# Bucket attention, experts and MLP on one core: the order of transposes and products of P in the attention

## The chip, the cores and the metric

The kernel runs on one core of a Trainium2 chip. The metric is the device time of one execution in microseconds (us). Two kernels are told apart by the ratio of their times over several runs.

## The reference

Three layers follow each other. What the change touches is the first one, an attention with a mask by hash buckets:

```
q, k, v: (2, 8, 768, 64) float32;  proj: (64, 6)
q_bucket, k_bucket = sum over 6 bits of 2**i * ((q or k) @ proj > 0)
scores = q @ k.T / 8, and -1e9 where the buckets of a query and a key differ
attn   = exp(scores - rowmax);  attn /= sum(attn) + 1e-9
x      = attn @ v, heads side by side: (1536, 512)
```

Then a layer of eight experts: a token goes to the expert with the largest router logit (x @ w_gate + a bias by modality), and its output is gate * relu(x @ w1[e]) @ w2[e]. Then an MLP: softplus(x @ w_in) @ w_out with 2048 inner columns. All results are float32, and the kernel computes products in two float32r parts (a high part H and the rest L), so that they are close to float32.

## The kernel before, in words

**Groups and pieces.** The attention works through 48 groups. A group is 256 queries of one head: two tiles of 128. For each tile, TensorE makes scores (pieces S0 and S1, four products each, a tile of two PSUM banks), VectorE takes the row maximum (M0, M1), GpSimd makes scale and bias of the exponent from it, and ScalarE makes the exponentials P with their sums (X0, X1).

P has its queries on the partitions, and the product with v needs its keys there. So TensorE transposes P, 128 x 128 at a time, into PSUM tiles `ps_t` of which there are two. A *bank* is one such tile: two tiles of keys for two tiles of queries, four transposes; a group has three banks (T0, T1, T2). ScalarE casts a bank to P's high part PH (H0, H1, H2), and VectorE subtracts it to get the low part PL (L0, L1, L2). Both read the `ps_t` tile, so it is free for another bank when its L is done.

The product with v (V0, V1, V2, by bank) has v as the stationary operand and PH or PL as the moving one, 256 columns (the two tiles of queries). v is held as 128 columns a head: 64 of its high part and 64 of its low part. PH meets all 128 (a *full* product), PL the 64 of the high part alone (a *narrow* product). For each of the two tiles of keys of a bank the order is full, narrow; the group's last tile of keys has them the other way round. All accumulate in one PSUM tile `ps_o`. ScalarE copies it to SBUF (O), TensorE adds its two halves and gives the router's logits with products of 72 columns (F, four records, into columns that the tile of S1's scores leaves free), and VectorE scales the result by the sums (r).

**Iterations.** Pieces of different groups are interleaved. In iteration `it` the scores are those of group `it`, the transposes those of group `it - 2`, the products with v those of group `it - 3` and F, O and r those of group `it - 4`. Up to iteration 40 there is also R, a piece of the next head pair's preparation (transposes of q or k, or products for the bucket bits), with its readers A on ScalarE and D on VectorE. Each engine has an order of its own, written out by hand:

```
ORDER = ("S0 T0 V0 T1 S1 F V1 T2 R V2", "O X1 H0 H1 X0 H2 A", "M0 L0 M1 L1 r L2 D")
```

These are the orders of TensorE, ScalarE and VectorE. `FIRST` has such lines for iterations 0 to 5, and `DRAIN` for the last four groups and the first work of the experts behind them. `run` and the loop over `DRAIN` issue a piece when those that it needs have been issued (`after`, `needs`); they wait for nothing at run time beyond semaphores for data and buffers. From iteration 28 on some pieces of the routing run in between on VectorE, TensorE and GpSimd.

After the attention come the routing, the experts' slots with their weights split into two parts by ScalarE and VectorE, and the MLP. Lines to follow: `scores` L242, `rowmax` L254, `expo` L265, `tpose_pe` L274 (transposes, L283), `tpose_hi` L286 (L288), `tpose_lo` L290 (L293), `pv` L296 (products, L307), `fin1` L310 (L313), `fin_pe` L323 (L329), `fin_dve` L331 (L338, L344), `prep_pe` L154 (L175).

Of the kernel before, what the change touches and what calls it, by code (L numbers as in the profile page):

```python
# [15 lines left out]
PSUM = bass.MemoryType.PSUM  # L16
P = 128
BIG = 4096.0
RND = 1.5 * 2.0 ** 23  # added and subtracted, it rounds a float32 to the nearest integer
OFF = (P - 1) / 2  # L20


class Attention:
    """Bucket-masked attention, a pair of heads at a time.

    q and k are transposed and split into float32r parts H + L. One K=128 product of [qH; qH] with
    [kH; kL] and one of [qL; bits] with [kH; bits] give the scores: the bit rows add exactly 0 for
    equal buckets and at most -1 (of scores scaled by 2**-32) for others. A row without a match
    has its exponent scaled by 0.
    """  # L30
# [19 lines left out]
    def open(self, ctx, c_p):  # L50
        """ctx: for the whole of the attention; c_p: a pool for constants"""
        self.c_p = c_p
        # what the last pair needs until its operands are made lies on top, and goes first
# [9 lines left out]
        # and so goes what the pair before it takes  # L63
# [37 lines left out]
    # products of zeros: the tensor engine's clock is up when the first operands come  # L101
# [17 lines left out]
    def consts_c(self):  # L119
        nc, c_p, D = self.nc, self.c_p, self.D  # L120
        # sums the two parts of the output, and gives its share of the router logits
        self.wgx = c_p.tile([P, self.H, D + self.E], F32, name="wgx")
        for i in range(2):
            sl = slice(D * i, D * i + D)
            nc.vector.tensor_copy(self.wgx[sl, :, :D], self.ident[sl, sl].unsqueeze(1).to_broadcast([D, self.H, D]))
            nc.scalar.dma_start(out=self.wgx[sl, :, D:], in_=self.wg.rearrange("(h d) e -> d h e", d=D))
# [27 lines left out]
    def prep_pe(self, m, i, ps_of=None):  # L154
        nc, S, HS = self.nc, self.S, self.HS
        if i == 0:
            own = ("qH", "qL", "kH", "kL", "bt")
            self.prep[m] = {}
            if m == 0:
                # in the place of tiles that come later, so that the next pair's need not wait  # L160
# [57 lines left out]
    def head0(self, i):  # L218
        """the first head's operands by the engines, which have nothing else to do yet"""
# [54 lines left out]
    def tpose_pe(self, g, bk):  # L274
        e = self.st[g]
# [4 lines left out]
        for kk in range(2):  # L280
            for t in range(2):
                kt = 2 * bk + kk
                self.nc.tensor.transpose(ps[:, kk, t], e["P"][t][:, kt * P:(kt + 1) * P], self.ident)  # L283
        e["T", bk] = ps.rearrange("p k t n -> p (k t n)")

# [10 lines left out]
    def pv(self, g, bk):  # L296
        m, j, u = self.gm(g)
        e = self.st[g]
        if bk == 0:
            e["O"] = self.ps_m.tile([P, 512], F32, tag="o", name="ps_o")  # L300
        O, vh, NT = e["O"], self.vhl[m], self.NT
        for kt in (2 * bk, 2 * bk + 1):
            ops = [(P, "PH"), (self.D, "PL")]
            if kt == NT - 1:
                ops.reverse()
            for n, nm in ops:
                self.nc.tensor.matmul(O[:n, :2 * P], vh[:, j, kt, :n], e[nm][:, kt], start=(kt == 0 and n == P),  # L307
                                      stop=(kt == NT - 1 and n == P))
# [8 lines left out]
    def spare(self, s):  # L317
        """the columns that a tile of scores leaves free in its two banks, [P, 2, P]"""
# [35 lines left out]
    def run(self, aside, aside_ps, end):  # L354
        """the groups, up to iteration end"""
# [17 lines left out]
        for t in range(4):  # L373
            self.split_v(0, t)
        after = {"M0": ["S0"], "M1": ["S1"], "X0": ["M0"], "H0": ["T0"], "H1": ["T1"], "H2": ["T2"], "L0": ["H0"],
                 "L1": ["H1"], "L2": ["H2"], "F": ["O", "S1"], "R": ["M1"], "r": ["F"], "A": ["R"], "D": ["A"], "S1": ["S0"], "T0": [], "T1": ["T0"],
# [5 lines left out]
        for it in range(end):  # L382
# [7 lines left out]
            # the second pair's operands are made with the first group, while nothing else can be done  # L390
# [6 lines left out]
            def do(k):  # L397
# [9 lines left out]
                elif a == "T" and ok(T_):  # L407
                    self.tpose_pe(T_, n)
                elif a == "H" and ok(T_):
# [20 lines left out]
                # the second pair's operands  # L430
# [31 lines left out]
    # per iteration: the order of the pieces on PE, ACT and DVE  # L462
    LAG = (2, 3, 4)
    ORDER = ("S0 T0 V0 T1 S1 F V1 T2 R V2", "O X1 H0 H1 X0 H2 A", "M0 L0 M1 L1 r L2 D")
    # the first iterations, p, a and d being the second pair's pieces on PE, ACT and DVE
# [11 lines left out]
class Moe:  # L477
    def __init__(self, tc, ctx, ident, mid, wg, mb, w1, w2, win, wout, x_dram, x2_dram, out):
# [10 lines left out]
        # slots: as many as the experts' tokens can take, and the first NA of them, that are always computed  # L489
        self.NS = self.TT + self.E - 1  # L490
        self.NA = self.NS - 2
        # and the first two once more
# [11 lines left out]
    def consts(self, e_p):  # L504
        """a generator; e_p: a pool for what is used up here"""
# [29 lines left out]
        # row of x2 of each slot row, if the slots were full  # L535
# [3 lines left out]
        # id of token b * 768 + p * 6 + t as 64 * (high + 32) + low  # L539
# [19 lines left out]
        # tri[k, m] = 1 where k < m  # L559
# [40 lines left out]
    def bias(self, m):  # L600
        """logits start as the bias of the token's modality: the share of modality m"""
# [29 lines left out]
    # A token takes the slot row slotbase[expert] * 128 + rank, the rank counting its expert's tokens before it.  # L631
    # The generators yield where an engine may do other things in between.
    def route_a(self, b):
        """the expert of each token of batch b, one-hot, and the exponentials that its gate takes"""
# [34 lines left out]
    def ranks(self, R, t0, t1):  # L669
        """adds the ranks that the tokens of columns t0 to t1 bring; R: [P, t, E] of PSUM"""  # L670
# [6 lines left out]
    def place(self, src, t0, t1):  # L677
        """slot (relative where src has no slot bases) and row of the tokens of columns t0 to t1, the row as (row - OFF) / 128"""
# [17 lines left out]
    def gate3(self, eng, t0, t1):  # L696
        """gates as three bfloat16 parts"""
# [11 lines left out]
    # The first slot holds the first tokens of the expert that most tokens of batch 0 go to, and the second one more of them:  # L709
    # where batch 0 has more than 128 of them, as is all but sure, its product can run before batch 1 is done.  # L710
    # Elsewhere it and the second slot write nothing, and come again after the other slots.
    def first_a(self, ps):
        """ranks modulo 128 of batch 0, and its most frequent expert; ps: [P, 2, P] of PSUM"""
# [26 lines left out]
    def first_b(self):  # L740
        """what its tokens bring to the table of the first slot"""
# [24 lines left out]
    def first_c(self):  # L766
        """the order of the experts with that one in front"""
        E, tp, G = self.E, self.tp, self.nc.gpsimd
        # nothing is written by the first two slots
# [11 lines left out]
        # tri[k, m] = 1 where k comes before m  # L781
# [20 lines left out]
    def first_d(self, ps):  # L802
        """token and gate of the first slot's rows; ps: [P, 2, P] of PSUM"""
# [31 lines left out]
    def route_n(self, i):  # L835
        """the slots that come before each expert, into the ranks"""
# [13 lines left out]
        if i == 3:  # L850
            # for the tables that are not needed at once
# [9 lines left out]
    def open_route(self):  # L861
        """the pools on the right that the experts take"""
# [747 lines left out]
```

## Time and profile before

| | |
|---|---|
| median of 3 runs | 784.7 us (782.81 to 785.21) |
| span of the profiled execution | 782.7 us |
| TensorE: products busy / weight loads busy | 757.3 us (97%) / 646.5 us (83%) |
| VectorE, ScalarE, GpSimd busy | 588.3 us (75%), 521.0 us (67%), 282.0 us (36%) |
| attention, about | 5 to 260 us |

The profile was taken from one execution; its own device time is not listed beside the span, and the median of the runs lies 2.0 us above that span. PE is TensorE's row of products and transposes, PEld its row of weight loads, DVE is VectorE, ACT ScalarE and POOL GpSimd. TensorE's instructions overlap: a record opens before the one ahead of it has ended, so the time that one costs is the distance between starts and not the length of a record. Where equal instructions follow each other they stand merged in the timeline, with their first start, the time from that start to the last end, and their count.

### The profile page before, as it was taken

Reading aid. Unit: us, or ns where it says so; the run is one execution under the profiler, and the core shown is the slowest. Engines: PE = TensorE matmul, PEld = TensorE weight load, DVE = VectorE, ACT = ScalarE, POOL = GpSimd, SP = SyncE. Lnnn points to the kernel's source line nnn. Section 1 sums busy time; section 2 is a strip of 40 time slices with the busy share of each in tenths; the row PEclk is TensorE's granted clock in tenths of the full one; section 3 lists DMA queues with packets and bytes.
Section 4 is the critical chain, followed back from the end, with each engine's and each line's share of the span. In section 5 each row is a group of like instructions: output and inputs, shape, how many; then the busy total and the mean of one; then the engine's idle time right before and its main releaser. Section 6 shows DMA issues by size and latency. Waiting matters only on the chain. (4 is left out here: it accounts for less than half of the span.)

```text
span 782.7 us, 13113 instructions
## 1 busy us (share of the span) xinstructions
PE 757.3 (97%) x4225; PEld 646.5 (83%) x4225; DVE 588.3 (75%) x842; ACT 521.0 (67%) x869; POOL 282.0 (36%) x627
## 2 busy tenths in 40 slices
PE   7899999999999999999999999999989999999996
PEld 5799999999999767878878888766668888888874
DVE  6798888898988868999999998899973333433250
ACT  5787787887879568898898898555553333342340
POOL 4455544446565564234432133544441100020001
PEclk9999999999999989999999999999999999999999
DMA  8855647526660013679963642244430100010001
GB/s 195 186 129 121 162 94 165 149 63 170 181 198 22 21 41 130 216 245 340 370 241 110 209 156 68 88 161 165 162 107 24 40 1 1 27 54 1 0 1 54
DMA packets 72602, 95.28 MB, mean 122 GB/s; under 512 B 31843, under 2 KB 48227, under 8 KB 72529
## 3 DMA queue, kind: packets, MB, share of 16 engines
q1 hardware_dynamic: 67152, 83.85, 36.2%
q0 software_dynamic: 3744, 9.45, 3.4%
q10 hardware_dynamic: 1632, 1.08, 0.6%
q8 instruction: 35, 0.57, 0.3%
q14 instruction: 39, 0.31, 0.1%
HBM read 105.18 MB, written 10.76 MB: 148 GB/s over the span
## 5 line engine op out<-in xcount | busy, mean ns | idle before, releaser
L997 DVE TENSOR_TENSOR wL<-wr,wH 128x1024 fp32r<-128x1024 f32 (+1 forms) x134 | 160.9, 1232 | 13.2 <-ACT wH L992 12.9
L992 ACT CAST wH<-wr 128x1024 fp32r<-128x1024 f32 (+1 forms) x144 | 141.4, 1005 | 7.4 <-PE ps_p L1113 2.8
L1304 DVE SCALAR_TENSOR_TENSOR gg<-ps_f,ga 128x512 f32<-128x512 f32 x48 | 33.0, 689 | 108.0 <-ACT ga L1300 108.0
L260 DVE TENSOR_REDUCE mx<-s 128x1 f32<-128x768 f32 x96 | 91.6, 954 | 21.8 <-PE s L329 19.3
L271 ACT ACTIVATE p<-s,nb,sc 128x768 f32<-128x768 f32 x96 | 96.0, 1000 | 15.7 <-POOL nb L262 12.8
L293 DVE TENSOR_TENSOR PL<-ps_t,PH 128x512 fp32r<-128x512 f32 x144 | 98.3, 683 | 7.0 <-ACT PH L288 6.7
L1298 ACT ACTIVATE ga<-ps_f 128x512 f32<-128x512 f32 x48 | 28.7, 598 | 107.1 <-PE ps_f L1296 107.1
L288 ACT CAST PH<-ps_t 128x512 fp32r<-128x512 f32 x144 | 83.9, 589 | 16.6 <-PE ps_t L283 14.1
L250 PE MATMUL s<-K,Q 76*128 76x384 f32 (+1 forms) x384 | 88.2, 350 | 2.4 <-ACT p L271 0.9
L307 PE MATMUL ps_o<-PH,vhl 128*128 128x256 f32 x288 | 86.7, 316 | 0.6 <-ACT Os L313 0.6
L283 PE MATMUL ps_t<-ident,p 128*128 128x128 f32 x576 | 86.4, 272 | 0.6 <-DVE PL L293 0.6
L1296 PE MATMUL ps_f<-x2H,mwL 128*128 128x512 f32 x192 | 77.1, 402 | 3.2 <-POOL mwL L1285 3.2
L1296 PE MATMUL ps_f<-x2H,mwH 128*128 128x512 f32 x192 | 77.1, 401 | 0.1
L1331 PE MATMUL ps_o<-mwH,gL 128*128 128x512 f32 x192 | 76.9, 401 | 0.0
L1296 PE MATMUL ps_f<-x2L,mwH 128*128 128x512 f32 x192 | 76.1, 396 | 0.0
L1331 PE MATMUL ps_o<-mwH,gH 128*128 128x512 f32 x192 | 75.8, 395 | 0.0
L1331 PE MATMUL ps_o<-mwL,gH 128*128 128x512 f32 x192 | 75.8, 395 | 0.0
L283 PEld LDWEIGHTS ps_t<-ident,p 128*128 128x128 f32 x576 | 69.4, 140 | 2.7 <-PE s L250 0.9
L1285 POOL TENSOR_TENSOR mwL<-w,mwH 128x1024 fp32r<-128x1024 f32 x16 | 47.6, 2978 | 62.4 <-ACT mwH L1284 62.4
L307 PE MATMUL ps_o<-PL,vhl 128*64 128x256 f32 x288 | 68.3, 280 | 0.0
L250 PEld LDWEIGHTS s<-K,Q 76*128 76x128 f32 (+1 forms) x384 | 62.9, 189 | 4.0 <-ACT p L271 1.7
L1125 POOL DMA_INDIRECT x_dram<-y,cpi x17 | 23.8, 1397 | 102.1 <-ACT y L1120 70.9
(292 smaller groups left out, 1663.2 us busy)
## 6 DMA issues: line engine op xcount, KB each, us to landing
wr<-in_moe_w_dram SPq DMA_DIRECT2D x136, 512.0 KB
wraw<-in_moe_w_in_dram SPq DMA_DIRECT2D x16, 512.0 KB
wraw<-in_moe_w_out_dram SPq DMA_DIRECT2D x16, 512.0 KB
Q<-qH SPq DMA_DIRECT2D x28, 192.0 KB
K<-kH SPq DMA_DIRECT2D x28, 192.0 KB
rawv<-in_v_dram SPq DMA_DIRECT2D x8, 384.0 KB
x_dram<-x SPq DMA_DIRECT2D x8, 384.0 KB
rawq<-in_q_dram SPq DMA_DIRECT2D x14, 192.0 KB
```

The costliest lines, as they stand in the source:

```text
L250: self.nc.tensor.matmul(s[:, h, :HS], d[l, j][:kk, ts], d[r, j][:kk, h * HS:(h + 1) * HS], start=(a == 0), stop=(a == 1))
L260: nc.vector.tensor_reduce(mx, s[:, :, :self.HS], axis=AX.XY, op=ALU.max)
L271: self.nc.scalar.activation(e["P"][ti].rearrange("p (h c) -> p h c", h=2), s[:, :, :self.HS], AF.Exp, scale=sc, bias=nb, accum_out=e["sum" ...
L283: self.nc.tensor.transpose(ps[:, kk, t], e["P"][t][:, kt * P:(kt + 1) * P], self.ident)
L288: self.nc.scalar.copy(e["PH"][:, 2 * bk:2 * bk + 2].rearrange("p k n -> p (k n)"), e["T", bk])
L293: self.nc.vector.tensor_tensor(e["PL"][:, sl].rearrange("p k n -> p (k n)"), e["T", bk], e["PH"][:, sl].rearrange("p k n -> p (k n)").bitc ...
L307: self.nc.tensor.matmul(O[:n, :2 * P], vh[:, j, kt, :n], e[nm][:, kt], start=(kt == 0 and n == P), stop=(kt == NT - 1 and n == P))
L992: self.nc.scalar.copy(self.wt[s, c][0][:, sl], self.raw[c][:, sl])
L997: eng.tensor_tensor(L[:, sl], self.raw[c][:, sl], H[:, sl].bitcast(F32), op=ALU.subtract)
L1285: nc.gpsimd.tensor_tensor(L, w, H.bitcast(F32), op=ALU.subtract)
L1296: nc.tensor.matmul(ps, w[:, 0, sl], x[:, k], start=(k == 0 and n == 0), stop=(k == self.KD - 1 and n == 2))
L1331: nc.tensor.matmul(self.ops[i], a[:, sl], w[:, 1], start=(f == 0 and n == 0), stop=(f == NF - 1 and n == 2))
```

## The change

Transposes and products of a bank are issued in another order. A new piece W stands for T and V of the same number in one: two transposes, then the bank's four products in their order, each narrow one with a transpose straight ahead of it. So where the order was T T T T full narrow full narrow, it is T T full T narrow full T narrow (in a group's last bank T T full T narrow T narrow full). The transposes are those of group `it - 2`, the products those of group `it - 3`, as before. TensorE's order by iteration has W0, W1 and W2 in place of T and V; with that V1 stands ahead of S1 and F, and R behind the last bank. In `DRAIN` a T that a V follows is issued so too, where that V can be issued, and some V's are moved up behind a T. Comments are dropped.

```diff
     def tpose_pe(self, g, bk):
+        for f in self.tposes(g, bk):
+            f()
+
+    def tposes(self, g, bk):
...
+        def one(kk, t):
+            kt = 2 * bk + kk
+            self.nc.tensor.transpose(ps[:, kk, t], e["P"][t][:, kt * P:(kt + 1) * P], self.ident)
+        return [lambda kk=kk, t=t: one(kk, t) for kk in range(2) for t in range(2)]
+
+    def tpose_pv(self, gt, gv, bk, bv=None):
+
+        ts = self.tposes(gt, bk)
+        ts.pop(0)()
+        ts.pop(0)()
+        for narrow, f in self.pvs(gv, bk if bv is None else bv):
+            if narrow:
+                ts.pop(0)()
+            f()
...
     def pv(self, g, bk):
+        for _, f in self.pvs(g, bk):
+            f()
+
+    def pvs(self, g, bk):
...
+        def one(kt, n, nm):
+            self.nc.tensor.matmul(O[:n, :2 * P], vh[:, j, kt, :n], e[nm][:, kt], start=(kt == 0 and n == P),
+                                  stop=(kt == NT - 1 and n == P))
+        made = []
         for kt in (2 * bk, 2 * bk + 1):
             ops = [(P, "PH"), (self.D, "PL")]
             if kt == NT - 1:
                 ops.reverse()
...
+            made += [(n < P, lambda kt=kt, n=n, nm=nm: one(kt, n, nm)) for n, nm in ops]
+        return made
...
+                elif a == "W":
+                    self.tpose_pv(T_, V_, n)
...
-    ORDER = ("S0 T0 V0 T1 S1 F V1 T2 R V2", "O X1 H0 H1 X0 H2 A", "M0 L0 M1 L1 r L2 D")
+    ORDER = ("S0 W0 W1 S1 F W2 R", "O X1 H0 H1 X0 H2 A", "M0 L0 M1 L1 r L2 D")
...
-        3: ("S0 T0 V0 T1 S1 V1 T2 V2", "X1 H0 H1 X0 H2", "M0 L0 L1 M1 L2"),
-        4: ("T0 S0 V0 T1 S1 F V1 V2 T2", "O X1 H0 H1 X0 H2", "M0 L0 M1 L1 r L2"),
-        5: ("S0 T0 V0 T1 S1 F V1 T2 R V2", "O X1 H0 H1 X0 H2 A", "M0 L0 M1 L1 r L2 D"),
+        3: ("S0 W0 W1 S1 W2", "X1 H0 H1 X0 H2", "M0 L0 L1 M1 L2"),
+        4: ("W0 S0 W1 S1 F W2", "O X1 H0 H1 X0 H2", "M0 L0 M1 L1 r L2"),
+        5: ("S0 W0 W1 S1 F W2 R", "O X1 H0 H1 X0 H2 A", "M0 L0 M1 L1 r L2 D"),
...
-    "S04 T02 V01 T12 S14 F0 V11 T22 V21 S05 T03 V02 T13 S15 F1 V12 T23 V22 S06 T04 V03 V13 T14 S16 F2 T24 x0 V23 S07 T05 V04"
-    " T15 S17 F3 V14 T25 V24 g00 T06 V05 T16 F4 V15 V25 T26 T07 g01 V06 T17 V16 T27 V26 F5 g10 V07 F6 V17 V27 g11 F7 E g20 g21"
+
+    "S04 T02 V01 T12 V11 S14 F0 T22 V21 S05 T03 V02 T13 V12 S15 F1 T23 V22 S06 T04 V03 T14 V13 S16 F2 T24 x0 V23 S07 T05 V04"
+    " T15 V14 S17 F3 T25 V24 g00 T06 V05 T16 V15 F4 V25 T26 T07 g01 V06 T17 V16 T27 V26 F5 g10 V07 F6 V17 V27 g11 F7 E g20 g21"
...
+                if k[0][0] == "T" and len(k) > 1 and k[1][0] == "V" and all(y in done for y in needs(k[1])):
+                    (bt, gt), (bv, gv) = ([int(x) for x in y[1:]] for y in k[:2])
+                    att.tpose_pv(NG - 2 * TAIL + gt, NG - 2 * TAIL + gv, bt, bv)
+                    done.add(k.pop(0))
+                else:
+                    do(k[0])
```

## Rows read from the trace of the kernel before

**Rows 1.** Busy time by engine in a stretch: stretch, its length, then each engine.

```profile
200.00:250.00 50.00, 50.00 (x396) 49.45 (x395) 43.74 (x80) 43.20 (x89) 29.17 (x105) 1.00 0.50 137
```

**Rows 2.** TensorE's waits, 30 to 255 us: total us, times, longest.

```profile
PE ps_o L307 <- ACT Os L313: 0.6, 1, 0.6
```

**Rows 3.** Timeline of TensorE, iteration 44, without R: start us, us, what.

```profile
235.59 0.87 PE L250 MATMUL s<-K,Q 128*128 128x384 f32 x4
236.29 0.60 PE L283 MATMUL ps_t<-ident,p 128*128 128x128 f32 x4
236.65 0.36 PE L307 MATMUL ps_o<-PH,vhl 128*128 128x256 f32 x1
...
237.08 0.28 PE L307 MATMUL ps_o<-PL,vhl 128*64 128x256 f32 x1
237.20 0.60 PE L283 MATMUL ps_t<-ident,p 128*128 128x128 f32 x4
...
238.37 0.56 PE L329 MATMUL s<-wgx,Os 128*128 128x72 f32 x4
...
239.28 0.60 PE L283 MATMUL ps_t<-ident,p 128*128 128x128 f32 x4
...
240.19 0.86 PE L250 MATMUL s<-K,Q 128*128 128x384 f32 x4
```

**Rows 4.** Groups by line and shape, 150 to 330 us: busy us, mean ns.

```profile
L283 PE MATMUL ps_t<-ident,p 128*128 128x128 f32 x268 | 40.1, 272 | 0.0
...
L329 PE MATMUL s_spare<-wgx,Os 128*128 128x72 f32 x16 | 2.4, 274 | 0.0
...
L283 PEld LDWEIGHTS ps_t<-ident,p 128*128 128x128 f32 x268 | 32.2, 141 | 0.8
L307 PEld LDWEIGHTS ps_o<-PH,vhl 128*128 128x128 f32 x142 | 26.8, 189 | 0.3 <-ACT Os L313 0.2
L307 PEld LDWEIGHTS ps_o<-PL,vhl 128*64 128x64 f32 x142 | 18.9, 136 | 0.0
```

**Rows 5.** Timeline of all engines, iteration 37, with a short R.

```profile
200.47 0.88 PE L250 MATMUL s<-K,Q 128*128 128x384 f32 x4
...
200.81 0.68 DVE L293 TENSOR_TENSOR PL<-ps_t,PH 128x512 fp32r<-128x512 f32 x1
...
202.10 0.60 PE L283 MATMUL ps_t<-ident,p 128*128 128x128 f32 x4
...
205.39 0.34 PE L250 MATMUL s<-K,Q 128*128 128x384 f32 x1
```

**Rows 6.** Timeline of two narrow windows, transposes after an idle stretch.

```profile
22.43 0.14 PEld L283 LDWEIGHTS ps_t<-ident,p 128*128 128x128 f32 x1 [0.88 <-PE s L250]
...
22.46 0.41 PE L283 MATMUL ps_t<-ident,p 128*128 128x128 f32 x2 [0.58 <-DVE PL L293]
22.49 0.25 PEld L283 LDWEIGHTS ps_t<-ident,p 128*128 128x128 f32 x2
```

**Rows 7.** Timeline of a narrow window, scores after an idle stretch.

```profile
19.74 0.30 PEld L250 LDWEIGHTS s<-K,Q 128*128 128x128 f32 x2 [0.41 <-ACT p L271]
```

**Rows 8.** Timeline of TensorE, narrow window, F straight behind a transpose.

```profile
256.43 0.38 PE L283 MATMUL ps_t<-ident,p 128*128 128x128 f32 x2
256.65 0.34 PE L329 MATMUL s_spare<-wgx,Os 128*128 128x72 f32 x2
```

**Rows 9.** Timeline of VectorE, iteration 44, without R.

```profile
236.26 0.68 DVE L293 TENSOR_TENSOR PL<-ps_t,PH 128x512 fp32r<-128x512 f32 x1
...
238.97 0.96 DVE L260 TENSOR_REDUCE mx<-s 128x1 f32<-128x768 f32 x1 [0.25 <-PE s L329]
...
240.86 0.68 DVE L293 TENSOR_TENSOR PL<-ps_t,PH 128x512 fp32r<-128x512 f32 x1
```

**Rows 10.** Timeline of all engines, iteration 32, with routing work.

```profile
175.26 0.68 DVE L293 TENSOR_TENSOR PL<-ps_t,PH 128x512 fp32r<-128x512 f32 x1
...
176.03 0.29 PE L283 MATMUL ps_t<-ident,p 128*128 128x128 f32 x1
```

More of the change, by code (lines that the diff above doesn't have):

```diff
@@ L279, in tpose_pe @@
         ps = self.ps_t.tile([P, 2, 2, P], F32, tag="t", name="ps_t")
[L280 to L283, printed above, removed]
         e["T", bk] = ps.rearrange("p k t n -> p (k t n)")
+        def one(kk, t):
[10 more added lines that the diff above has]
+            f()
     def tpose_hi(self, g, bk):
@@ L305, in pv @@
                 ops.reverse()
-            for n, nm in ops:
-                self.nc.tensor.matmul(O[:n, :2 * P], vh[:, j, kt, :n], e[nm][:, kt], start=(kt == 0 and n == P),
-                                      stop=(kt == NT - 1 and n == P))
+            made += [(n < P, lambda kt=kt, n=n, nm=nm: one(kt, n, nm)) for n, nm in ops]
+        return made
     def fin1(self, g):
@@ L374, in run @@
             self.split_v(0, t)
-        after = {"M0": ["S0"], "M1": ["S1"], "X0": ["M0"], "H0": ["T0"], "H1": ["T1"], "H2": ["T2"], "L0": ["H0"],
-                 "L1": ["H1"], "L2": ["H2"], "F": ["O", "S1"], "R": ["M1"], "r": ["F"], "A": ["R"], "D": ["A"], "S1": ["S0"], "T0": [], "T1": ["T0"],
+        after = {"M0": ["S0"], "M1": ["S1"], "X0": ["M0"], "H0": ["T0", "W0"], "H1": ["T1", "W1"], "H2": ["T2", "W2"], "L0": ["H0"],
+                 "L1": ["H1"], "L2": ["H2"], "W1": ["W0"], "W2": ["W1"], "F": ["O", "S1"], "R": ["M1"], "r": ["F"], "A": ["R"], "D": ["A"], "S1": ["S0"], "T0": [], "T1": ["T0"],
                  "T2": ["T1"], "V1": ["V0"], "V2": ["V1"], "X1": [], "X0": ["M0", "X1"], "M1": ["S1", "M0"], "V0": [], "p4": ["d0", "d1"]}
@@ L1569 @@
                 k = next(x for x in todo if x and all(y in done for y in needs(x[0])))
-                do(k[0])
+                if k[0][0] == "T" and len(k) > 1 and k[1][0] == "V" and all(y in done for y in needs(k[1])):
[4 more added lines that the diff above has]
+                    do(k[0])
                 done.add(k.pop(0))
```

## The prediction

> **What bounds the kernel now.** The busy times by stretch come first: in the attention TensorE is busy all the time, while VectorE works 87% of it and ScalarE 86% [rows 1]. Busy is not yet bound, so the waits come next: from 30 to 255 us TensorE's longest wait for a compute engine totals 0.6 us, beside one for a load of constants [rows 2]. So the attention (about 5 to 260 us) lasts as long as TensorE's instructions take one after the other, and the question is what an instruction adds to that row of starts. The timeline answers it. Four transposes are one record of 0.60 us; with 272 ns for one [rows 3, 4] that makes (600 - 272) / 3 = 109 ns from start to start. Products with a moving operand of 256 columns start every 0.11 to 0.12 us, narrow (64 weight columns) or full (128) [rows 3]; I take 117 ns. One bank of four transposes and four products is therefore 4 x 109 + 4 x 117 = 904 ns, and between the starts of the first two transpose groups I read 237.20 - 236.29 = 0.91 us [rows 3].
>
> An iteration holds three such banks, two tiles of scores, the output step F and, up to iteration 40, a piece of the next pair's preparation (R). With a short R its period is 205.39 - 200.47 = 4.92 us [rows 5]; without R 240.19 - 235.59 = 4.60 us [rows 3]. Two iterations in six have a longer R.
>
> **The change, part by part.** No instruction is added or removed: 48 groups of three banks still issue 576 transposes and 576 products, ScalarE, VectorE and GpSimd keep their orders, and no DMA moves. Two things change: who follows whom inside a bank, and where the second bank's four products (V1) stand in the iteration.
>
> *Who follows whom.* Before: T T T T full narrow full narrow. After: T T full T narrow full T narrow. Product after product, transpose after transpose and product to transpose are known: 117, 109 and, from 237.08 to 237.20, 0.12 us [rows 3]. Not in the trace is a narrow product straight behind a transpose; a transpose always has 128 weight columns behind it. The bound from below: could the transpose stream its operand in less than 109 ns, the narrow product could start as soon as its weights are in. The nearest row is a transpose's own load, behind which the next one starts 22.49 - 22.43 = 0.06 us later [rows 6]. That saves 50 ns, twice a bank, 288 times: at most 14.4 us. From above: today's bank, with one switch to products and one back, is read as 0.91 us where the sum is 904 ns, so a switch costs up to 6 ns: 288 x 6 = 1.7 us.
>
> Which end? What matters is whether a transpose's 109 ns are its weight load or its stream. Three rows say stream. After an idle stretch the second load starts those 0.06 us after the first, so the loader is free; yet the second transpose starts only at 22.46 + 0.41 - 0.27 = 22.60, another 0.11 us later [rows 6]. After an idle stretch before scores, two loads make 0.30 us, so with 189 ns each the second starts 0.11 us after the first [rows 7]: there a load does take that long. The load records agree: 141 ns for a transpose's 128 columns, like 136 for 64 columns of v and unlike 189 for 128 of v [rows 4]. And a transpose followed by F's product: the transpose starts at 256.43 + 0.38 - 0.27 = 256.54, the first F record at 256.65, 0.11 us later; the second F record opens 0.34 - 0.27 = 0.07 us after the first [rows 4, 8], less than the 0.11 of a full load, so F's records open when the stream ahead is through, and the transpose's took 0.11. So I take the upper end: a narrow product gains nothing behind a transpose, and two extra switches a bank cost 2 ns each, a third of the bound, 288 x 2 = 0.6 us.
>
> The Trainium skill's page "TensorE: Matmul & The Clock Gate", section "LDWEIGHTS (loading the stationary operand)", puts a load at columns / 1.2 ns, whatever the kind. By it a transpose would be bound by its 107 ns load, a narrow load would take 53, and 54 x 288 = 15.6 us of TensorE's time would go: the mechanism of the first rival below. The transposes' rows do not agree with it (0.06 us against 0.11 for the scores).
>
> *Where V1 stands.* V1 moves from behind F to before the second scores S1. S1 and F are later by one V1: F starts at 238.37, the next transposes at 239.28, 0.91 us for F and V1 together, of which four products are 0.47 us. S1's row maximum on VectorE (M1) waits for F: F's record ends at 238.37 + 0.56 = 238.93, M1 starts at 238.97 [rows 3, 9]. So M1 is 0.47 us late, and behind it, in order and without idle time, stand L1, the two small output operations and L2. They end the reading of the transposes' two PSUM buffers: three banks an iteration on two buffers, so next iteration's first transposes wait for L1, its second ones (T1) for L2.
>
> Today's slack of T1 behind L2: with R 202.10 - (200.81 + 0.68) = 0.61 us [rows 5]; without R 237.20 - (236.26 + 0.68) = 0.26 us [rows 3, 9]; in the iteration at 174 us, where routing work shares VectorE, 176.03 - (175.26 + 0.68) = 0.09 us, which I take as about what the signal itself needs [rows 10]. With R, 0.61 - 0.47 = 0.14 us are left: still hidden, with 0.05 to spare. Without R, 0.26 - 0.47 is negative: a new wait. Its size follows from the loop that now closes: F's end to M1 0.04, M1 to L2's end 240.86 + 0.68 - 238.97 = 2.57, signal 0.08, then on TensorE bank 1 with V1 0.91, S1 0.71 (S0's 236.29 - 235.59), F 0.56: 4.87 us, against 4.60. So 0.27 us an iteration, for six iterations (their waits fall in 42 to 47): 1.6 us. In the iteration of [rows 10] all 0.47 us come through; three others (5, 31 and 39) have less than the 0.55 needed, an estimate of 0.1 to 0.4 us each: 1.1 us together.
>
> H0 and H1 (ScalarE's casts) come 0.35 us later, since the last transpose of a bank now stands seventh of eight; ScalarE's 14% of idle time [rows 1] hides that, and if it did not, the next wait would be S0's for the exponentials. R moves behind V2, 0.47 us later; its readers A and D come last on their engines, so nothing waits for them.
>
> Sum: 0.6 + 1.6 + 1.1 = 3.3 us, on the profiled span of 782.7 us 786.0. The runs' median lies 2.0 us above that span, so 788.0; I predict 787.8 us. The attention's last groups feed the routing, which feeds everything after, so I pass its delay on whole. About 0.3%, 2.35 us, is what a measurement of this kernel can tell from no change: the forecast lies barely beyond it.
>
> **Rivals.** *The narrow load hides behind the transpose* (other side: faster). A transpose to a narrow product takes 60 ns: 0.30 us an iteration off TensorE. For it speaks that the first full product's record opens 0.03 us behind a transpose (236.65, the transpose at 236.29 + 0.60 - 0.27 = 236.62 [rows 3]), as if the stream were free; against it the three rows above. It would not all arrive: the loop has two 50 ns steps in its bank, 4.77 us. The some 23 short iterations with R would fall by 0.15 us, the 12 long ones by about 0.25, together 6.4; the six without R still rise by 0.17, the crowded ones cost 0.7: 784.7 - 6.4 + 1.0 + 0.7 = 780.0 us. Decides from: under 85 ns from a transpose to a narrow product. Chance 15%.
>
> *The lateness is absorbed*: M1 follows S1 rather than F, or VectorE catches up. VectorE's 0.25 us idle time before M1 speaks for it [rows 9], M1's release by F against it. Then 0.6 us remain: 785.3 us. It decides where T1's wait is under 0.1 us without R. Chance 23%.
>
> *A narrow product behind a transpose makes the array run empty first*: 272 - 109 = 163 ns, 288 times, 47 us: 832 us. Against it: the way back, narrow to transpose, costs 0.12 us as any product does [rows 3]. Decides from 130 ns for the step. Chance 4%. Here "TensorEngine Tiling (Array Packing)", section "Tiling Modes" of the Trainium skill, says that changing the tiling mode drains TensorE. Full and narrow products alternating every 0.11 to 0.12 us show no such drain.
>
> **How the numbers follow.** The forecast has 58%. Its own range is 786 to 792: waits between half of 2.7 and twice that, switches from 0 to 1.7 us. With the absorbed case that makes 81%; the range from 781 to 793 us holds both and stops at the edge of the first rival. Slower: 0.7 of the forecast and the drain, 0.45, and 0.48 with the last iterations, which share VectorE with the experts' first weights. Within 0.3%: the rest of the forecast, 0.17, and most of the absorbed case, 0.37. Faster: the first rival, 0.15.
>
> **What would show it.** Right: a bank in the attention still 0.90 to 0.92 us, a transpose to a narrow product 107 to 115 ns; iterations with R at 4.92 us, those from 42 on at 4.8 to 4.9; among TensorE's waits a new one for L2 (VectorE, PL), 1.5 to 4 us in total. Wrong: a step of 60 to 85 ns, banks of 0.80 us; or F no longer releasing M1; or waits that fall elsewhere, on S0 for the exponentials.

## The result and the profile after

The changed kernel takes 789.45 us (median of 6 runs, 787.68 to 790.99) where the kernel before takes 783.5 us (6 runs, 780.26 to 785.21). The ratio is 1.0074, 95% interval 1.0055 to 1.0093: slower, by 0.0074 x 783.5 = 5.8 us. The forecast was 787.8 us, so direction and range hold. It started from a kernel before of 784.7 us, whose median over six runs is 783.5: of the change it foresaw 3.1 us, and 5.8 were measured.

TensorE's busy time first, in the stretch of [rows 1] (stretch, length, PE, PEld, DVE, ACT, POOL, granted clock, DMA share, GB/s):

```profile
200.00:250.00 50.00, 49.59 (x380) 46.59 (x379) 42.74 (x80) 41.36 (x85) 27.23 (x102) 1.00 0.53 150
```

It still looks full, with 380 instructions instead of 396. The waits from 30 to 255 us, as in [rows 2], with those of the weight loads (PEld):

```profile
PEld ps_o L323 <- ACT Os L336: 3.9, 11, 2.3
...
PE ps_o L323 <- ACT Os L336: 2.1, 1, 2.1
...
PEld ps_t L289 <- PE s L250: 1.2, 3, 0.5
...
PEld s L250 <- ACT p L271: 0.8, 2, 0.5
...
PEld ps_t L289 <- DVE PL L309: 0.3, 1, 0.3
```

The list names O (ScalarE's copy of a finished group out of `ps_o`, now line 336), and hardly L2, which the forecast had named. The list is short for two reasons: a product's record opens before the one ahead of it has ended, so that a short wait disappears in the overlap on PE's row; and the list has only idle times of more than 0.15 us, so that of the waits of 0.14 to 0.16 us that the weight loads show in most iterations with a short R it counts a few. So I compared the starts of S0, iteration by iteration:

```
                              before         after
most with a short R           4.91 - 4.92    5.05 - 5.07
first short R behind a long   4.89 - 4.93    4.78 - 4.80
most with a long R, first     5.64 - 5.66    5.87 - 5.93
most with a long R, second    5.62 - 5.65    5.58 - 5.59
iterations 41 to 46 together  27.99          29.52
S0 of iteration 6 to 47       209.71         215.07
```

The two profiled spans differ by 788.9 - 782.7 = 6.2 us. The stretch from S0 of iteration 6 to S0 of iteration 47 holds 5.36 of it, the start 2.06 (S0 of iteration 6 at 42.10 instead of 40.05), and what comes behind it gives back 1.2.

**A short-R iteration after the change**, which answers to [rows 5]. ScalarE's timeline (start, us, what):

```profile
200.29 0.59 ACT L304 CAST PH<-ps_t 128x512 fp32r<-128x512 f32 x1
200.85 0.49 ACT L187 ACTIVATE qH<-ps_prep 128x384 fp32r<-128x384 f32 x1
201.24 0.37 ACT L336 COPY Os<-ps_o 128x256 f32<-128x256 f32 x1
```

The same iteration on TensorE, its weight loads:

```profile
201.28 0.22 PEld L289 LDWEIGHTS ps_t<-ident,p 128*128 128x128 f32 x2
201.66 0.19 PEld L323 LDWEIGHTS ps_o<-PH,vhl 128*128 128x128 f32 x1 [0.16 <-ACT Os L336]
...
201.99 0.19 PEld L323 LDWEIGHTS ps_o<-PH,vhl 128*128 128x128 f32 x1
202.12 0.14 PEld L289 LDWEIGHTS ps_t<-ident,p 128*128 128x128 f32 x1
202.23 0.14 PEld L323 LDWEIGHTS ps_o<-PL,vhl 128*64 128x64 f32 x1
202.34 0.26 PEld L289 LDWEIGHTS ps_t<-ident,p 128*128 128x128 f32 x2
```

and its products:

```profile
199.98 0.27 PE L289 MATMUL ps_t<-ident,p 128*128 128x128 f32 x1
...
200.32 0.49 PE L175 MATMUL ps_prep<-ident,rawq 128*128 128x128 f32 x3
200.57 0.95 PE L250 MATMUL s<-K,Q 128*128 128x384 f32 x4
...
202.46 0.38 PE L289 MATMUL ps_t<-ident,p 128*128 128x128 f32 x2
...
203.37 0.85 PE L250 MATMUL s<-K,Q 128*128 128x384 f32 x4
204.06 0.56 PE L352 MATMUL s<-wgx,Os 128*128 128x72 f32 x4
204.46 0.38 PE L289 MATMUL ps_t<-ident,p 128*128 128x128 f32 x2
...
205.38 0.49 PE L175 MATMUL ps_prep<-ident,rawk 128*128 128x128 f32 x3
205.62 0.42 PE L250 MATMUL s<-K,Q 128*128 128x384 f32 x1
```

Two things are to be seen. From a transpose's load to that of the narrow product behind it there are 202.23 - 202.12 = 0.11 us, and 0.11 more to the next transpose's (202.34); an undisturbed bank is 203.37 - 202.46 = 0.91 us, as before the change. And bank 0's first product, the first of a new group in `ps_o`, waits for O, which ends at 201.24 + 0.37 = 201.61; O waits for A (line 187) in ScalarE's order, and A for R's transposes. In the kernel before the same place has room (timeline of all engines, the load of the same product last):

```profile
199.87 0.59 ACT L288 CAST PH<-ps_t 128x512 fp32r<-128x512 f32 x1
...
200.36 0.50 ACT L187 ACTIVATE kH<-ps_prep 128x384 fp32r<-128x384 f32 x1
...
200.74 0.38 ACT L313 COPY Os<-ps_o 128x256 f32<-128x256 f32 x1
...
201.52 0.19 PEld L307 LDWEIGHTS ps_o<-PH,vhl 128*128 128x128 f32 x1
```

O ends there at 201.12, 0.40 us ahead of that load. The change takes 2 x 0.11 = 0.22 us of it, since the first product now stands behind two transposes and not four. The rest goes because O ends later: 201.61 - 200.57 = 1.04 us behind the start of S0, where it was 201.12 - 200.47 = 0.65.

These 0.39 us are not R's alone. Ahead of A stands the cast H2, and it starts 0.04 us behind the last transpose of the mixed bank (199.98 + 0.27 = 200.25, then 200.29): 0.28 us ahead of S0, where it was 200.47 - 199.87 = 0.60. In the kernel before, A follows H2 by 200.36 - 199.87 = 0.49 us. So had R been done earlier, A could have started at 200.29 + 0.49 = 200.78 instead of 200.85, an estimate: R releases A, but the late last transpose would hold it nearly as long.

### The profile page after: what moved, and what is told of

Its sections match the earlier page's. It is cut to its first block, busy times and chain, and to the rows that moved or that the text cites. A ratio compares the mean times of both kernels' runs of the same rounds, so it can differ in the third digit from the quotient of the medians.

```text
span 788.9 us, 13107 instructions
## 1 busy us (share of the span) xinstructions
PE 760.7 (96%) x4225; PEld 643.6 (82%) x4225; DVE 587.2 (74%) x842; ACT 525.7 (67%) x869; POOL 282.2 (36%) x627
## 5 line engine op out<-in xcount | busy, mean ns | idle before, releaser
L289 PE MATMUL ps_t<-ident,p 128*128 128x128 f32 x576 | 121.1, 275 | 1.0 <-DVE PL L309 0.6
L323 PE MATMUL ps_o<-PH,vhl 128*128 128x256 f32 x288 | 93.1, 325 | 2.1 <-ACT Os L336 2.1
L323 PE MATMUL ps_o<-PL,vhl 128*64 128x256 f32 x288 | 93.2, 353 | 0.0
L289 PEld LDWEIGHTS ps_t<-ident,p 128*128 128x128 f32 x576 | 75.1, 145 | 6.5 <-PE s L250 2.1
```

## The experiments

Each kernel is the changed one with the edit shown, unless it says otherwise; ratios are to the kernel before, with their intervals. "The stretch" is S0 of iteration 6 to S0 of iteration 47 in the profiled execution: 209.71 us before, 215.07 after.

**R back ahead of V2** (so the last bank isn't mixed):

```diff
-    ORDER = ("S0 W0 W1 S1 F W2 R", ...
+    ORDER = ("S0 W0 W1 S1 F T2 R V2", ...
...
```

> The changed kernel with its last bank not mixed and R back between T2 and V2 (iterations from 5 on); W0 and W1 stay. Theory O (in iterations with R the loss is the wait of a bank's first full product for ScalarE's copy O, which stands behind A, and A behind the late R): A and O come 0.4 us earlier, short-R iterations fall from 5.06 to 4.92 to 4.97 us, those without R stay at 4.7 to 5.1, time about 786 us. Theory M (all of the loss is the late row maximum M1, through L1 and L2): short-R iterations stay at 5.03 to 5.07, time 789 us.

788.54 us, ratio 1.0057 (1.0033 to 1.008), stretch 213.90. Short-R iterations alternate between 4.89 and 5.06. So about half of the short-R loss goes, less than expected, and in about every second iteration O still comes too late. In one of these (timeline of all engines):

```profile
204.22 0.49 PE L175 MATMUL ps_prep<-ident,rawk 128*128 128x128 f32 x3
...
204.67 0.19 ACT L271 ACTIVATION_READ_ACCUMULATOR p<-s,nb,sc 128x1 f32 x1
204.77 0.58 ACT L304 CAST PH<-ps_t 128x512 fp32r<-128x512 f32 x1
...
205.23 0.50 ACT L187 ACTIVATE kH<-ps_prep 128x384 fp32r<-128x384 f32 x1
...
205.62 0.38 ACT L336 COPY Os<-ps_o 128x256 f32<-128x256 f32 x1
...
206.05 0.19 PEld L323 LDWEIGHTS ps_o<-PH,vhl 128*128 128x128 f32 x1 [0.18 <-ACT Os L336]
```

R has ended at 204.71, and A starts only at 205.23, 0.46 us behind H2. H2 starts 0.38 us behind the last transpose of its bank but 0.10 behind the exponential's last step (204.67). So here it is the exponential that makes O late.

**V1 back behind F**, banks 0 and 2 still mixed:

```diff
-    ORDER = ("S0 W0 W1 S1 F W2 R", ...
+    ORDER = ("S0 W0 T1 S1 F V1 W2 R", ...
...
```

> The changed kernel with V1 back behind F, so that bank 1 is not mixed (T1 S1 F V1); W0, W2 and the late R stay. Theory O: short-R iterations stay at about 5.0 to 5.06 us, since R, A and O stay where they are; the iterations without R fall from 4.65 to 5.07 to 4.60 to 4.65; time about 787 us. Theory M: short-R iterations fall to 4.92 too, time 785 us.

789.84 us, ratio 1.0067 (1.0041 to 1.0094), stretch 214.80; the time is no better than the changed kernel's, where 787 was expected. Iterations 41 to 44 are back (4.57 4.65 4.64 4.60, 18.46 us together where before has 18.41), the short-R ones are not (5.10 to 5.12). The load of bank 0's first product in one of them:

```profile
201.57 0.19 PEld L323 LDWEIGHTS ps_o<-PH,vhl 128*128 128x128 f32 x1 [0.16 <-ACT Os L336]
```

Two losses, then: V1's place costs where there is no R, and something else costs where there is. They touch, though: the exponential's last step comes 1.00 us ahead of S0 or earlier in these short-R iterations, and 0.45 ahead in most of the changed kernel's. So V1's place makes it late, and with R early that is what holds O (the run above).

**The places without the mixing**: W issues four transposes and then the four products.

```diff
-        ts = self.tposes(gt, bk)
-        ts.pop(0)()
-        ts.pop(0)()
-        for narrow, f in self.pvs(gv, bk if bv is None else bv):
-            if narrow:
-                ts.pop(0)()
-            f()
+        self.tpose_pe(gt, bk)
+        self.pv(gv, bk if bv is None else bv)
```

> The changed kernel's places for V1 and R, but in each W the four transposes first and then the four products, so that no product of v's high part with PL's follows a transpose. If a narrow product gains nothing behind a transpose, a bank stays at 0.90 to 0.92 us; the first product of bank 0 then stands 0.22 us later behind the start of T0, so the wait for O goes: short-R iterations 4.92 to 4.97 us, those without R still 4.8 to 4.9, time 785 to 787 us. If narrow products do gain behind a transpose, banks become longer here by 0.05 to 0.1 us and the time goes up to 792 us or more.

787.47 us, ratio 1.0038 (1.0013 to 1.0063), stretch 212.24. Short-R iterations 4.89, those without R as in the changed kernel (29.55 us for 41 to 46). The short-R loss needs the mixing.

**The mixing without the places**: W0, and the transposes of the last bank mixed with V1's products where both stood side by side already; R, FIRST and the drain as before.

```diff
+                elif a == "Y":
+                    self.tpose_pv(T_, V_, 2, 1)
...
-    ORDER = ("S0 W0 W1 S1 F W2 R", ...
+    ORDER = ("S0 W0 T1 S1 F Y R V2", ...
...
```

> The mixing alone: bank 0 mixed (W0), V1 mixed with the transposes of bank 2 behind F, R and V2 as in the kernel before; the first iterations and the drain as before. If mixing itself neither gains nor costs, iterations are 4.92 us with a short R and 4.60 without, time that of the kernel before within 0.3% (781 to 786 us). If narrow products gain behind a transpose: 4.70 to 4.80 us, time 776 to 779 us. If switches between transposes and products cost more than 5 ns each: 4.96 us or more, 785 to 787 us.

783.3 us, ratio 0.9992 (0.9973 to 1.0012), stretch 209.66. Run again, beside the last two experiments below:

> The kernel with the mixing of the last bank alone, again, beside the one above on the same chip. If the mixing by itself neither gains nor costs: ratio 0.998 to 1.001 to before, iterations 4.88 to 4.91 and 4.57 to 4.65 us. If the load of a narrow product were hidden behind a transpose: 0.1 us a bank less in this bank, 48 banks, some 5 us, ratio 0.994.

784.53 us, ratio 1.0008 (0.9991 to 1.0025), stretch 209.66. The mixing by itself neither gains nor costs as a whole: in both runs most iterations are some 0.02 us shorter, and 14, 31 and 32 are 0.15 to 0.26 longer. (The second expectation counts the last bank alone; two banks an iteration are mixed in this kernel, so that a hidden load would have gained twice what it says.)

**A full product behind the transpose instead of the narrow one**:

```diff
-            if narrow:
+            if not narrow:
```

> The changed kernel, but the third and fourth transpose of a bank stand ahead of the full products in place of the narrow ones (T T T full narrow T full narrow). If it makes no difference which product follows a transpose, a bank without waits stays at 0.91 us; bank 0's first product stands 0.11 us later, so its wait for O shrinks from 0.19 to about 0.08 us and short-R iterations go from 5.06 to 4.92 to 4.98 us, those without R stay; time 786 to 788 us. If narrow products behind transposes do save something, banks grow by 0.05 to 0.1 us and the time stays at 789 us or rises.

788.67 us, ratio 1.006 (1.0043 to 1.0078), stretch 214.11; a bank again takes 0.91 us, and O is waited for some 0.1 us an iteration (4.99 to 5.00, a little more than expected). Here the first product stands behind three transposes. With four (no mixing) the wait is gone, with three the period is 0.10 us over 4.89, with two 0.16 to 0.18: the loss follows the place of bank 0's first product.

**The old order in FIRST alone, in the drain alone**: iterations 3 to 5 as before (the first of their lines is shown); then the last groups' order as before, without mixing there.

```diff
-        3: ("S0 W0 W1 S1 W2", ...
...
+        3: ("S0 T0 V0 T1 S1 V1 T2 V2", ...
...
```

> The changed kernel with the first six iterations of the kernel before (FIRST not mixed, iteration 5 included). If the new order of the first iterations costs the 1.4 to 2 us by which iteration 6 starts later in the changed kernel's profile, the time falls to 787 to 788 us and the rest of the iterations stay (5.06 with a short R). If the delay there is only a matter of when the constants' load lands, which differs from run to run, nothing is gained: 789 us.

790.51 us, ratio 1.0061 (1.0033 to 1.009), S0 of iteration 6 at 42.77 us.

```diff
-    "S04 T02 V01 T12 V11 S14 F0 T22 V21 ...
+    "S04 T02 V01 T12 S14 F0 V11 T22 V21 ...
...
```

> The changed kernel with the drain of the kernel before (its order and no mixing there). If the late row maximum is what costs the iterations without R, those of the drain (44 to 46) fall from 4.9 to 5.2 us back to 4.60 to 5.0, 0.8 to 1.0 us in all, and the time to about 788.5 us; if what is lost there is given back by the end of the drain anyway, as the shorter rest of the changed kernel's profile suggests (531.7 against 532.9 us behind the last scores' start), the time stays at 789 us.

788.35 us, ratio 1.0051 (1.0031 to 1.007); iterations 44 to 46 together 14.69 us (after 15.09, before 14.18). The drain's order is worth 0.4 us of the stretch. FIRST's order does not explain the late start of iteration 6: with the old one iteration 6 begins at 42.77 here and at 39.83 in the mixing-only kernel, with the new one between 39.83 and 42.56 over the other runs.

**O ahead of A**: TensorE's order untouched; ScalarE copies the group that has just been finished before it takes R's result.

```diff
-                elif a == "O" and ok(F_):
-                    self.fin1(F_)
+                elif a == "P" and ok(V_) and V_ < NG - 8:
+                    self.fin1(V_)
...
-    ORDER = ("S0 W0 W1 S1 F W2 R", "O X1 H0 H1 X0 H2 A", ...
+    ORDER = ("S0 W0 W1 S1 F W2 R", "X1 H0 H1 X0 H2 P A", ...
...
```

> The changed kernel with ScalarE's copy O moved: it is issued at the end of the iteration whose V2 it reads, ahead of A, and not behind A at the start of the next. TensorE's order is untouched. Theory O: the wait of bank 0's first product goes, short-R iterations fall from 5.06 to 4.89 to 4.95 us, 3 to 4 us in all, time 785 to 786.5 us; those without R stay, since they have no A. Theory M: the waits for L1 and L2 remain and take its place, short-R iterations stay above 5.0 us, time 788 to 789 us.

785.87 us, ratio 1.0018 (0.9998 to 1.0039), stretch 211.78. All engines at O, with the load that waited at the end:

```profile
201.29 0.38 ACT L336 COPY Os<-ps_o 128x256 f32<-128x256 f32 x1
...
201.56 0.51 ACT L187 ACTIVATE kH<-ps_prep 128x384 fp32r<-128x384 f32 x1
...
201.72 0.22 PEld L289 LDWEIGHTS ps_t<-ident,p 128*128 128x128 f32 x2
...
201.91 0.19 PEld L323 LDWEIGHTS ps_o<-PH,vhl 128*128 128x128 f32 x1
```

The wait for O is gone and the short-R iterations are at 4.89 to 4.90, with V1 and R where the change put them. Of the stretch's 5.36 us, 215.07 - 211.78 = 3.29 were O behind A. The iterations without R stay slow (29.59 us for 41 to 46).

**The account closed**: O ahead of A, V1 back behind F, the drain's old order; mixing in banks 0 and 2, R behind V2.

```diff
-    ORDER = ("S0 W0 W1 S1 F W2 R", "O X1 H0 H1 X0 H2 A", ...
+    ORDER = ("S0 W0 T1 S1 F V1 W2 R", "X1 H0 H1 X0 H2 P A", ...
...
```

> The mixing stays in banks 0 and 2. The product of the low part that belongs to bank 1 goes back behind F (so L1 is no longer late), ScalarE takes O for the just finished group ahead of A, and the drain's order is the old one without mixing. Theory (two waits and nothing else: O behind A, and the late L1/L2 of bank 1 moved ahead): iterations with a short R 4.88 to 4.91 us, iterations without R 4.57 to 4.65, the stretch from the start of iteration 6's scores to iteration 47's 209.4 to 210.2 us (before 209.71, after 215.07), so the time is within 0.3% of before. Rival (a third cause in the mixing itself, such as the alternation of 128 and 64 stationary columns): the stretch stays at 211 us or more and the ratio at 1.002 or more.

784.58 us, ratio 1.0008 (0.9991 to 1.0026), stretch 210.29, 0.09 us above the range expected. Short-R iterations are at 4.90 to 4.92, those without R at 4.59 to 4.64 up to 45 (46, in the drain, 4.97 as before the change) but for one of 5.15, iteration 42, where the scores wait for their operand's DMA:

```profile
227.75 0.59 PE L250 MATMUL s<-K,Q 76*128 76x384 f32 x2 [0.32 <-DMA Q<-bt]
```

The same wait is in the kernel with O ahead of A. Q's bucket bits come out of the preparation. R's place alone does not bring this wait: the kernel with V1 back has R there too, and its iteration 42 takes 4.65. What the two kernels with the wait share is that A stands behind O, 0.46 to 0.47 us behind the start of S0 and not 0.28; whether that is the cause was not tried. That iteration has 5.15 - 4.62 = 0.53 of the 0.58 us that are left over the kernel before.

**Transposes behind F's two products as well**, in the mixing-only kernel (F T F T and then full, T, narrow, T):

```diff
+                elif a == "Z":
+                    ts = self.tposes(T_, 2)
+                    self.fin_pe(F_, ss.get(1), ts)
+                    self.tpose_pv(T_, V_, 2, 1, ts)
...
-    ORDER = ("S0 W0 T1 S1 F Y R V2", ...
+    ORDER = ("S0 W0 T1 S1 Z R V2", ...
...
```

> Only the mixing of the last bank, and one transpose behind each of F's two products as well (F T F T, then full, T, narrow, and so on); the banks 0 and 1 and all other places as before. Theory (F's records are held by their weight loads, about 110 ns for a stream of 62, and a transpose's load is about 55): TensorE gains 0.05 to 0.1 us an iteration beyond the mixing alone, iterations with a short R 4.80 to 4.86 and without R 4.52 to 4.58, 2 to 4 us in all, ratio to before 0.995 to 0.998. Rival (the transposes of the last bank now come ahead of the rest of F, wait for the second exponential or hold F back, so r and M1 are late): 4.89 and 4.60 as before or up to 0.1 more, ratio 0.999 to 1.003.

792.11 us, ratio 1.0108 (1.0088 to 1.0128), short-R iterations 5.07 to 5.11. Its waits from 30 to 255 us:

```profile
PEld ps_t L289 <- DVE PL L309: 8.4, 38, 0.5
```

and one of them among the weight loads:

```profile
200.12 0.14 PEld L289 LDWEIGHTS ps_t<-ident,p 128*128 128x128 f32 x1 [0.17 <-DVE PL L309]
```

The rival took it: the last bank's transposes, one F earlier, wait for bank 0's L0, 38 times. Without that wait an estimate gives 5.09 - 0.17 = 4.92 us, no gain either. No version was found that is faster than the kernel before.

## Why the prediction was right or wrong

**A narrow product behind a transpose: right.** The step is 0.11 us and the bank 0.91, where the rival that hides the load asked for less than 85 ns and the draining one for at least 130. The two runs of the mixing alone bear it out: the stretch moves by 209.66 - 209.71 = -0.05 us, and not by the 41 x 2 x 0.10 = 8.2 us that the first rival's step would have saved in two banks of each iteration. Of the 0.6 us for switches nothing is to be seen. The Trainium skill's page "TensorE: Matmul & The Clock Gate", section "LDWEIGHTS (loading the stationary operand)", with its columns / 1.2 ns for a load, would by the forecast's estimate have saved 54 ns a step and made a bank 0.80 us; this trace does not agree, with 0.91.

**V1 ahead of S1: right in the cause and nearly in size, but by other waits.** Iterations 41 to 46 rose by 29.52 - 27.99 = 1.53 us, forecast 1.6. Taking V1 back brings 41 to 44 back. Iteration 32, beside routing work, rose from 4.94 to 5.39, 0.45 us where 0.47 was forecast. There L2 and the load of T1's first transpose stand so in the timeline of all engines:

```profile
180.33 0.68 DVE L309 TENSOR_TENSOR PL<-ps_t,PH 128x512 fp32r<-128x512 f32 x1
...
181.06 0.20 PEld L289 LDWEIGHTS ps_t<-ident,p 128*128 128x128 f32 x2 [0.32 <-DVE PL L309]
```

The load follows L2's end by 181.06 - (180.33 + 0.68) = 0.05 us, after an idle 0.32: the one entry of L2 in the list of waits. Of the three other crowded iterations that the forecast priced at 0.1 to 0.4 us each, 5 rose by 0.05, 31 by 0.21 and 39 by 0.28, the last two with a wait for O in them. The loop is less pure than forecast. In iteration 43, without R, three waits share it: S0 for an exponential, T0 for L1, T1 for L2 (timeline of all engines):

```profile
237.34 0.68 DVE L309 TENSOR_TENSOR PL<-ps_t,PH 128x512 fp32r<-128x512 f32 x1
237.36 0.65 PEld L250 LDWEIGHTS s<-K,Q 128*128 128x128 f32 x4 [0.23 <-ACT p L271]
...
238.13 0.20 PEld L289 LDWEIGHTS ps_t<-ident,p 128*128 128x128 f32 x2
...
238.35 0.68 DVE L309 TENSOR_TENSOR PL<-ps_t,PH 128x512 fp32r<-128x512 f32 x1
...
239.08 0.20 PEld L289 LDWEIGHTS ps_t<-ident,p 128*128 128x128 f32 x2
```

L1 ends at 238.02 and T0's load follows at 238.13; L2 ends at 239.03 and T1's at 239.08. In iteration 44 most of the wait stands at T0:

```profile
242.23 0.68 DVE L309 TENSOR_TENSOR PL<-ps_t,PH 128x512 fp32r<-128x512 f32 x1
...
243.02 0.20 PEld L289 LDWEIGHTS ps_t<-ident,p 128*128 128x128 f32 x2 [0.41 <-PE s L250]
```

L1 ends at 242.91, and the load follows 0.11 us later, as in iteration 43; the view puts the wait down to the scores ahead of it. This one and the like one of iteration 42 (0.35 us) are in the entry of 1.2 us above. At T1 the loads stand idle for 0.07 to 0.08 us behind L2 in iterations 42 to 46. So the late row maximum costs what the forecast said by another wait than it said: behind L1 and the exponentials, and hardly behind L2. The wait for the exponential is the one that it named "if it did not", after calling it hidden, and among its own signs of being wrong. The sign of proof that I had offered, L2 in the list of waits with 1.5 to 4 us, did not come: it has 0.3 us there.

**With a short R nothing was to change: wrong.** The step that failed is "R moves behind V2, 0.47 us later; its readers A and D come last on their engines, so nothing waits for them", and with it "ScalarE's 14% of idle time [rows 1] hides that", said of H0 and H1, where H2 of the last bank comes later too. ScalarE's order is a ring: A is the last of one iteration, and O the first of the next stands right behind it. O frees `ps_o`, and the mixing starts the next group's products 0.22 us sooner behind T0. The new loop, from the rows after: bank 0's first product to bank 1 0.80 (201.66 to 202.46), bank 1 0.91, S1 0.69, F 0.40, the last bank 0.92 (204.46 to 205.38), R to A 0.53 (200.32 to 200.85), A to O 0.39, O to the product 0.42: 5.06 us. TensorE's own row is 4.89, and the iterations last 5.05 to 5.07. Nothing in this loop has slack: A follows R's end by 0.04 us, the load O's end by 0.05, and the rest stands back to back. But other releasers are close: by the estimate above H2 would hold A only 0.07 us less than R does. With TensorE's order untouched, O ahead of A removes the loss, which shows that O's place behind A is needed for it; without the mixing it is gone too, and less mixing shrinks it. In the run without the mixing A starts as late against S0 (0.28 to 0.31 us behind it, here 200.85 - 200.57 = 0.28), so R's place is enough to make A late; that the mixed last bank would be nearly enough too is argued and not shown. The part of the forecast about L2 in these iterations, 0.14 us of slack left, holds: with O out of the way they are at 4.89 to 4.90.

**The sum.** In the stretch: O behind A 3.29 us, which the forecast lacked; V1's place with the drain's order 211.78 - 210.29 = 1.49; 0.58 with the one DMA wait. Together 5.36. The forecast had 3.3, of which 2.7 were for V1 and 0.6 for switches. So it is in part luck that the time came out so near: V1's place cost less than priced, the switches nothing, and a wait of 3.29 us that was in no term took their place. Between these two kernels iterations 41 to 46 differ by 29.59 - 28.56 = 1.03 us and the crowded 31 to 33 by 16.56 - 15.63 = 0.93; other iterations give half a microsecond back, which the forecast did not see. Against the medians the miss is smaller, 789.45 - 787.8 = 1.65 us, because the kernel before came out 1.2 us lower over six runs than over the three that the forecast started from.

**The first 40 us: a long wait and a fall of the clock.** The profiled execution lost 2.06 us there. Over the eleven experiments S0 of iteration 6 lies between 39.83 and 42.77 us, with either order in FIRST. The three profiles in which it comes latest (42.10, 42.56 with R back ahead of V2, 42.77 with the old FIRST) are the three in which the granted clock falls to 0.50 between 30 and 40 us. From S0 of iteration 3 to S0 of iteration 6 they take 17.9 to 18.2 us, all others 14.9 to 16.5. The kernel with the drain's old order, whose pieces stand in the same order up to there as in the changed kernel, takes 16.2 and shows no fall; of the 1.7 us between the two, 2.09 - 1.52 = 0.57 are its shorter wait for O. So one profile can't put these 2 us down to the change; whether the change makes the fall more frequent stays open.

## What to carry to other kernels

When a piece is moved, follow its reader and then whatever is queued behind that reader, around the end of the loop into the next iteration: the first piece of an engine's list waits for the last. Where several releasers end within 0.1 us of each other, undoing one of them gains only as far as the next. An order that starts a consumer earlier shortens the time that its buffer's last reader has, even where no duration changes. Where many waits of 0.1 to 0.2 us add up, compare starts from iteration to iteration; the list of waits shows only the longer ones.

## What the runs showed of the hardware

In the profiled execution of the changed kernel TensorE stood still for 2.09 us at the start, waiting for O, and its granted clock was lower afterwards. Its timeline:

```profile
30.91 0.44 PE L323 MATMUL ps_o<-PH,vhl 128*128 128x256 f32 x1 [2.09 <-ACT Os L336]
31.15 0.41 PE L289 MATMUL ps_t<-ident,p 128*128 128x128 f32 x1
```

and the stretches behind (columns as in the row for 200 to 250 us above):

```profile
32.00:33.00 1.00, 1.00 (x5) 1.00 (x5) 0.00 (x0) 0.59 (x1) 0.00 (x0) 0.50 0.10 8
33.00:34.00 1.00, 1.00 (x6) 0.90 (x5) 0.21 (x1) 0.00 (x0) 0.00 (x0) 0.50 0.00 0
34.00:35.00 1.00, 1.00 (x8) 1.00 (x8) 1.00 (x2) 0.03 (x1) 0.10 (x1) 0.75 0.83 181
```

0.50 is the lower level, 1.2 GHz, and the record of the transpose at 31.15 is 0.41 us instead of 0.27. The same is seen in two more profiles: with R back ahead of V2, TensorE stands still for 1.99 us for O, and the clock reads 0.50 from 32 to 34 us; with the old FIRST, 1.99 us for the load of constants, and 0.50 from 36 to 39 us:

```profile
34.37 0.64 PE L352 MATMUL s<-wgx,Os 128*128 128x72 f32 x4 [1.99 <-DMA wgx<-in_moe_w_gate_dram]
```

In the kernel before TensorE stands still for 1.45 us near the same place, for the load of constants, and the clock behind reads 1.00 (timeline, then the stretch):

```profile
33.08 0.64 PE L329 MATMUL s<-wgx,Os 128*128 128x72 f32 x4 [1.45 <-DMA wgx<-in_moe_w_gate_dram]
```

```profile
34.00:35.00 1.00, 1.00 (x12) 1.00 (x10) 1.00 (x2) 0.00 (x0) 0.06 (x1) 1.00 0.96 209
```

So a wait near the start can cost more than its own length. With V1 back and in one run of the mixing alone the clock also reads 0.50 to 0.52 from 14 to 16 us; what came ahead of that was not followed.
